# Block-sparse attention and a gated FFN: only batch 0 dense, three tokens to a partition, keys and queries turned by TensorE

## The chip, the cores and the metric

The kernel runs on one core of a Trainium2 chip. The metric is the device time of one execution in microseconds. A core has TensorE (PE: matmuls, with a separate weight load, PEld), VectorE (DVE), ScalarE (ACT), GpSimd (POOL) and the DMA issuing queue of SyncE (SP); ScalarE and GpSimd can issue DMAs too. Each engine works through its own instructions in the order in which they stand in the program, and waits on semaphores for the others. A DMA issue also waits for an older DMA that used the same semaphore, whichever engine issued that one.

## The reference

Attention over 4 batches, 8 heads, 768 tokens and 64 features per head; tokens are grouped in 24 blocks of 32. A query block sees its neighbours (one block to each side), the first and the last block, and three sampled blocks of its own. The first and the last query block see everything. Then an RMS norm and an FFN with a gate over all 3072 tokens:

```
mask = abs(blk_i - blk_j) <= 1  |  blk_i, blk_j in {0, 23}  |  sampled
attn = softmax(where(mask, q @ k.T / 8, -1e9));  o = attn @ v
x  = o as [3072, 512];  xn = x / rms(x) * rms_g
y  = (silu(xn @ w_gate) * (xn @ w_val)) @ w_out      # 512 -> 1536 -> 512
```

Inputs and output are float32; the kernel's matmuls take bfloat16.

## The kernel before

Two ways to do attention stand beside each other. A *dense* batch (`dk`, `dexp`, `dav`, `dxo`; L322, L343, L357, L370) computes all 768 x 768 scores of a head, with the mask added by 24 extra rows of the contraction (88 rows in all). A *sparse* batch computes, for each group of four query blocks (n = 0 to 4; n = 5, `AT`, is the group of the two full rows and two more blocks), the scores against gathered keys only (`qk` L599, `qka` L615, `exp` L605, `expa` L623, `av` L648, `xo` L659). `NDB = 2` batches are dense, two are sparse.

Keys and queries must have features on partitions. Batch 0's are turned by TensorE (`tpx`, L301) and evicted by `evx`. Batch 1's are cast into AUG and turned by a DMA transpose that SP issues (`turn`, L288). The sparse batches are loaded with a key or value layout of two tokens to a partition (`load_kv`, L452, 512-byte runs) and a query layout of one (`load_q`, L459, 256-byte runs), cast (`fill_k`, `fill_v`, `fill_q`) and turned by DMA transposes (`turn_k` L478, `turn_q` L504).

For each group of query blocks the keys are collected in a tile `kg`: neighbours and ends by `kg_fixed` (VectorE or ScalarE), sampled blocks by `kg_sampled` (POOL, L146), at places held in registers (`table`, `table_regs`, `k_at`). Values go to DRAM once in bfloat16 rows (`store_v`, L508) and come back by `pair_v` (L570 to L578, SP) and, for each sampled block, `block_v` (L555: two of three on SP, one on ScalarE).

The FFN takes units of 128 or 384 tokens (`UNITS`): `sq`, `rsq` (POOL, L686), `xq` (L693), then a turn of xn by TensorE for the first `NPET = 6` units (`tr` L704, `cp`) or by a DMA transpose (`xt`, L715), then gate and value projections (`proj`, L728), `th` (tanh on ScalarE, L737), `uu` and `hp` (VectorE, L743, L754) and the output projection `yy` (L767), `yo`, `so`.

The order is not written by hand: all steps are listed by `op(...)` with the engines that may do them, a cost for each, what they depend on, a priority and the buffers and PSUM banks that they take and give back. A greedy planner at the end of the function takes the step that can start first by those costs and issues its instructions. So the planner decides each engine's program order, and for some steps the engine. PSUM banks 0 to 3 in pairs serve scores, 4 and 5 gate and value projections, 6 the output projection, 7 attention output.

Of the kernel before, what the change touches and what calls it, by code (L numbers as in the profile page):

```python
# [10 lines left out]
I32 = mybir.dt.int32  # L11
# [5 lines left out]
def kernel(  # L17
# [33 lines left out]
    NSLOT, NAUG, NOPEN, NDB = 5, 2, 2, 2  # L51
    IXAT, RGAT = 36.0, 48.0
    NPT, NPA, NKG, NVG, NRAW = 4, 2, 2, 3, 3
    AHEAD, HURRY, HURU = 0.8, ("av", "xo", "sq", "rsq", "xq", "tr", "cp"), 0
    NSTARV, ZPAT, NG2 = 3, 32.0, 4
    AH = {"uu": 0.3, "hp": 0.3}
    WARM = (11, 10, 2)
    HD = NC * D // 2
    UNITS = [(0, 0, 1), (0, 1, 1), (0, 2, 1), (0, 3, 3)]
    UNITS += [(b, c, 3) for b in range(1, NDB) for c in (0, 3)]  # L60
    ND = len(UNITS)
    for b in range(NDB, B):
        UNITS += [(b, (5, 0, 1), 3), (b, (2, 3, 4), 3)]
    NU = len(UNITS)
    HG = [("h", 0 if u < 3 else u) for u in range(NU)]
    HO = [u if u < 3 else 0 for u in range(NU)]
# [9 lines left out]
    def bank16(n):  # L76
# [12 lines left out]
    VAC = const.tile([P, 2, H * NC, D + 2], BF16, name="VAC")  # L89
    VGC = const.tile([P, 6, VW], BF16, name="VGC")  # L90
# [6 lines left out]
    RAWD = list(A)  # L97
    RAWS = [RAWC[:, i * RB:(i + 1) * RB] for i in range(NRAW)]
    aug = [AUG[:, i] for i in range(NAUG)]
    va_ = [VAC[:, i] for i in range(2)]  # L100
    vfl = [t.rearrange("p m d -> p (m d)")[:, 0:6 * VW] for t in va_]
    VAUG = [t.rearrange("p (t c h d) -> p t c h d", t=NC // 2, c=2, h=H) for t in (vfl[0], PTC[:, 10240:10240 + 6 * VW])]
    rt_ = RAWC[:, NRAW * RB:].bitcast(BF16)
    VGB = [VGC, rt_[:, 0:6 * VW].rearrange("p (x w) -> p x w", w=VW),
           vfl[1].rearrange("p (x w) -> p x w", w=VW)]
    PD = [PTC[:, i * PDW:(i + 1) * PDW] for i in range(3)]
    PTB = [t.rearrange("p (h l x) -> p h l x", h=2, l=2) for t in [rt_[:, 6 * VW:6 * VW + 1024]] + [
        PTC[:, i * 1024:(i + 1) * 1024] for i in range(NPT - 1)]]
    PAB = [PTC[:, 3072 + i * 2048:3072 + (i + 1) * 2048].rearrange("p (l h x) -> p l h x", l=2, h=2) for i in range(NPA)]
    KTB = [t.rearrange("p (a s) -> p a s", a=NP) for t in (xs_[3], xs_[1])]  # L110
    QTB = [t.rearrange("p (a s) -> p a s", a=NP) for t in (xs_[4], PTC[:, 7168:7168 + NP * S])]
    KGB = [xs_[i].rearrange("p (x a s j c) -> p x a s j c", x=6, a=NP, s=4, j=16) for i in (0, 2)]
    KROW = AUG[:, 0].rearrange("p i e c x -> p (i e c x)").rearrange(
        "p (a c t x) -> p a c t x", a=NP, c=2, t=NC // 2)
    QROW = AUG[:, 1].rearrange("p i e c x -> p (i e c x)").rearrange("p (a n x) -> p a n x", a=NP, n=NC)
    kvv = [t.rearrange("b h (t p c) d -> b p (h t) (c d)", p=P, c=2) for t in (k, v)]
    qvv = q.rearrange("b h (n p) d -> b n p h d", p=P)
# [32 lines left out]
    zt = const.tile([P, VW], BF16, name="zt")  # L150
# [36 lines left out]
    nc.gpsimd.memset(zt[0:32, P:VW], 0.0)  # L187
# [9 lines left out]
    for t in va_:  # L197
        nc.vector.memset(t[:, :, D:D + 1], 1.0)
# [72 lines left out]
    def load(g, i):  # L271
        b, pr = divmod(g, NP)
        if i == 0:
            rawd[g] = RAWD[held["rawd", g][1]]
        nc.sync.dma_start(out=rawd[g][:, i], in_=(kv, qv, vv)[i][b, :, 2 * pr:2 * pr + 2, :])

    def fill(g, i, eng):
        copy(eng, aug[g % NAUG][:, i, :, :, 0:D],
             rawd[g][:, i].rearrange("p h (c d) -> p h c d", d=D))

    def pad_v(g, eng):
        b, pr = divmod(g, NP)
        src = rawd.pop(g) if b else A[g]
        copy(eng, va_[b][:, 2 * pr * NC:2 * (pr + 1) * NC, 0:D],
             src[:, 2].rearrange("p h (c d) -> p (h c) d", d=D))

    def turn(g):
        nc.sync.dma_start_transpose(  # L288
            out=X[g % NSLOT].rearrange("p i e (c t) -> p (i e c) t", t=P),
            in_=aug[g % NAUG].rearrange("p i e c r -> p (i e c r)"))  # L290

    def zero_pad(i):
        nc.vector.memset(aug[i][:, :, :, :, KQ:P], 0.0)
# [15 lines left out]
    held, rawd = {}, {}  # L309
# [38 lines left out]
    def dav(u, pr, bk):  # L348
        b, c0, nt = UNITS[u]
        pt, va = pts.pop((u, pr)), va_[b]  # L350
# [23 lines left out]

    tab_, at_ = VGB[0].rearrange("p x w -> p (x w)"), [0]

    def small(n, dt, p=P):
# [7 lines left out]
    kti, vti = small(NS * 2, I32, 1), small(NS * NR, I32, 1)  # L385
    koff, voff = {}, {}

    REGS = {"POOL": [("k", 0, 16), ("k", 16, 32), ("k", 32, 2 * NS)], "SP": [("v", 0, 16), ("v", 16, 32), ("v", 32, 2 * NS)],
            "ACT": [("v", 2 * NS, 2 * NS + 11), ("v", 2 * NS + 11, 3 * NS)]}
    HALF = 1024  # L390

    def load_table():
        nc.sync.dma_start(
            out=stab.rearrange("p n r i -> p (n r i)"), in_=s64.rearrange("n x -> (n x)").unsqueeze(0))
        for b in range(NDB, B):
            for lo in (0, S + 32):
                nc.sync.dma_start(out=vrows[b][lo:lo + 32, :], in_=zt[0:32, :])

    def table(i, eng):
# [3 lines left out]
        elif i == 1:  # L403
            TC(out=sf, in_=stab[:, 1:NB - 1, :, 0])
            TS(out=d2, in0=sf, scalar1=16.0, scalar2=None, op0=ALU.mult)
            TC(out=kti[:, 0:NS], in_=d2[:, :, 0])
            TS(out=d1[:, :, 0], in0=d2[:, :, 2], scalar1=float(HALF), scalar2=None, op0=ALU.mult)
            TT(out=kti[:, NS:2 * NS], in0=d1[:, :, 0], in1=d2[:, :, 1], op=ALU.add)
# [14 lines left out]
        else:  # L423

            TS(out=d2, in0=sf, scalar1=-1.0, scalar2=float(NB), op0=ALU.mult, op1=ALU.add)
# [6 lines left out]
    def table_regs(eng, part):  # L432
# [5 lines left out]
        for i_, x in enumerate(got_):  # L438
            r, n = divmod(lo + i_, NS)
            {"k": koff, "v": voff}[w][n * NR + r] = x  # L440
# [882 lines left out]
```

## Time and profile before

| what | value |
|---|---|
| median of 3 runs | 308.0 us (307.23 to 308.08) |
| profiled execution | 307.95 us, span 306.2 us |
| granted TensorE clock, mean | 0.989 |
| busy: PE, PEld, DVE, ACT, POOL | 284.4, 183.4, 195.1, 175.2, 80.3 us |
| HBM read, written | 36.70 MB, 8.02 MB |
| DMA packets on queue 1 | 76946, of them 256 B: 43008 |

How to read it: the span is the time from the first to the last instruction on the core; the profiled execution's own time is a little longer. Busy times of an engine count its instructions; register, branch, semaphore and DMA-issuing instructions are not among them. A line of the groups has the line of the kernel, the engine, the operation, out<-in with shapes, count, busy time and mean time of one. A line of the chain has start, length, engine, tile and line. A line of the waits has the engine and line, what it waited for, the total, the number of waits and the longest. A line of the windows has the stretch, its length, busy time of PE, PEld, DVE, ACT and POOL with counts, the granted clock, the DMA share and GB/s. A line of the timeline has start, length, engine, line, operation, tile and count, and in brackets the idle time before and what ended it.

### The profile page before, as it was taken

What the parts mean: (1) busy time and instruction counts of PE and PEld (TensorE: products, weight loads), DVE (VectorE), ACT (ScalarE), POOL (GpSimd) and SP (SyncE); (2) the same over time, 40 slices, a digit from 0 to 9 for tenths busy, and PEclk for the clock granted to TensorE, in tenths of its full rate; (3) what the DMA queues carried; (4) which work ended last, traced back from release to release, by engine and by line L of the source; (5) the groups of instructions that cost most, each with busy time, mean ns of one, the idle gap of its engine ahead of it and who ended that gap; (6) DMA issues with size and microseconds to landing.
All of it is one profiled execution on the core that took longest, in us unless ns stands there. A gap on an engine that the chain in (4) does not pass through costs nothing.

```text
span 306.2 us, 9818 instructions
## 1 busy us (share of the span) xinstructions
PE 284.4 (93%) x3838; PEld 183.4 (60%) x3838; DVE 195.1 (64%) x462; ACT 175.2 (57%) x290; POOL 80.3 (26%) x196
## 2 busy tenths in 40 slices
PE   8999989889999998999779699998699999999995
PEld 7899877666666664665445345564255655546543
DVE  6688896576756755877568435767177958807700
ACT  4899874468888785368554226877065424413322
POOL 4648100010024615119754200755041000100000
PEclk9999999999999999999999979999989999999999
DMA  7999999864799996783987973333754400060032
GB/s 218 364 242 157 203 268 323 182 229 80 119 267 266 182 308 161 159 239 87 263 196 187 195 157 97 90 84 89 166 127 135 92 36 2 0 156 0 1 98 109
DMA packets 85204, 48.50 MB, mean 158 GB/s; under 512 B 48037, under 2 KB 81318, under 8 KB 85158
## 3 DMA queue, kind: packets, MB, share of 16 engines
q1 hardware_dynamic: 76946, 41.63, 54.7%
q0 software_dynamic: 5792, 4.72, 10.1%
q10 hardware_dynamic: 2420, 1.53, 2.0%
q8 instruction: 30, 0.49, 0.6%
q14 instruction: 16, 0.13, 0.1%
HBM read 36.70 MB, written 8.02 MB: 146 GB/s over the span
## 4 chain that ended last, share of the span: by engine, by line
PE 67%; DMA 14%; DVE 8%; issue 5%; SPq 2%; ACT 2%; ACTq 1%; DVEq 0%
PE PS L728 33%; PE PS L767 15%; PE PS L322 7%; PE PS L357 4%; DMA RAWC<-in_v_dram 4%; PE PS L648 3%; DMA XC<-AUG 2%; DMA RAWC<-in_k_dram 2%; PE PS L301 2%; DMA VGC<-vrows 2%; DVE uu L743 2%; PE PS L599 2%; DMA xn<-xq 1%; DVE hp L754 1%; ACT th L737 1%
## 5 line engine op out<-in xcount | busy, mean ns | idle before, releaser
L737 ACT ACTIVATE th<-PS 128x384 bf16<-128x384 f32 x96 | 46.5, 492 | 81.9 <-PE PS L728 37.5
L743 DVE SCALAR_TENSOR_TENSOR uu<-th,PS 128x384 bf16<-128x384 bf16 x96 | 52.4, 551 | 49.4 <-ACT th L737 47.1
L728 PE MATMUL PS<-xn,wg 128*128 128x384 bf16 (+1 forms) x480 | 74.3, 294 | 7.3 <-DVE uu L743 4.2
L343 ACT ACTIVATE PTC<-PS 128x768 bf16<-128x768 f32 x92 | 70.4, 815 | 14.0 <-PE PS L322 13.8
L728 PE MATMUL PS<-xn,wv 128*128 128x384 bf16 (+1 forms) x480 | 77.9, 297 | 0.1
L767 PE MATMUL PS<-wo,hp 128*128 128x512 bf16 (+1 forms) x300 | 71.4, 376 | 4.1 <-DVE uu L743 4.1
L754 DVE TENSOR_TENSOR hp<-uu,PS 128x384 bf16<-128x384 bf16 x96 | 52.0, 551 | 16.8 <-PE PS L728 14.7
L728 PEld LDWEIGHTS <-wg 128*128 128x128 bf16 x480 | 40.7, 98 | 31.4 <-issue 9.0
L146 POOL COPY XC<-XC 128x128 bf16 x132 | 39.3, 371 | 62.6 <-PE PS L599 35.7
L728 PEld LDWEIGHTS <-wv 128*128 128x128 bf16 x480 | 40.5, 98 | 23.9 <-issue 1.9
L767 PEld LDWEIGHTS <-hp 128*128 128x128 bf16 x300 | 29.0, 99 | 32.4 <-issue 6.2
L322 PE MATMUL PS<-XC 88*128 88x128 bf16 (+1 forms) x288 | 42.6, 276 | 0.6 <-ACT PTC L343 0.6
L322 PEld LDWEIGHTS <-XC 88*128 88x128 bf16 x288 | 22.2, 100 | 7.8 <-issue 0.9
L357 PE MATMUL PS<-VAC,PTC 128*128 128x65 bf16 x552 | 21.1, 193 | 0.2 <-DVE XO L370 0.2
L357 PEld LDWEIGHTS <-PTC 128*128 128x128 bf16 x552 | 20.0, 97 | 2.0 <-issue 0.3
L777 ACT ACTIVATE yo<-PS 128x512 f32<-128x512 f32 (+1 forms) x16 | 9.1, 571 | 20.2 <-PE PS L767 20.1
L146 POOL CAST AUG<-RAWC 128x768 bf16<-128x768 f32 (+3 forms) x12 | 11.6, 973 | 30.1 <-DMA RAWC<-in_k_dram 25.7
L693 DVE SCALAR_TENSOR_TENSOR xq<-XO,rs,gB 128x512 bf16<-128x512 f32 x24 | 18.5, 792 | 0.2 <-POOL rs L686 0.2
L686 POOL TENSOR_TENSOR rs<-ms,nhalf 128x1 f32<-128x1 f32 (+1 forms) x6 | 4.3, 714 | 47.8 <-DVE ms L675 47.8
L605 ACT ACTIVATE PTC<-PS 128x1024 bf16<-128x1024 f32 x15 | 15.2, 1022 | 1.6 <-PE PS L599 1.1
L648 PEld LDWEIGHTS <-PTC 128*32 128x32 bf16 x736 | 8.1, 97 | 8.7 <-issue 7.4
L599 PEld LDWEIGHTS <-XC 64*128 64x128 bf16 x480 | 7.5, 93 | 6.9 <-issue 5.8
(112 smaller groups left out, 225.1 us busy)
## 6 DMA issues: line engine op xcount, KB each, us to landing
out_dram<-yo SPq DMA_DIRECT2D x21, 256.0 KB, 2.0
RAWC<-in_k_dram SPq DMA_DIRECT2D x4, 768.0 KB, 5.7
RAWC<-in_v_dram SPq DMA_DIRECT2D x4, 768.0 KB, 10.6
RAWC<-in_q_dram SPq DMA_DIRECT2D x12, 256.0 KB, 5.3
RAWC<-in_v_dram SPq DMA_DIRECT2D x7, 384.0 KB, 6.5
RAWC<-in_k_dram SPq DMA_DIRECT2D x6, 384.0 KB, 6.6
wg<-in_moe_w_gate_dram POOLq DMA_DIRECT2D x4, 384.0 KB, 6.9
wv<-in_moe_w_val_dram POOLq DMA_DIRECT2D x4, 384.0 KB, 7.9
```

The costliest lines, as they stand in the source:

```text
L146: nc.gpsimd.tensor_copy(out=out, in_=in_)
L322: nc.tensor.matmul(out=s_[:, e, j * w:(j + 1) * w], lhsT=x[0:KQ, 0, e, jt * P:(jt + 1) * P], rhs=x[0:KQ, 1, e, c0 * P:c0 * P + w], start=T ...
L343: nc.scalar.activation(out=pts[u, pr][:, g * kt:(g + 1) * kt].rearrange("p j e w -> p e j w"), in_=s_[:, :, 0:kt * w].rearrange("p e (j w) ...
L357: nc.tensor.matmul(out=o_[:, t, e, :], lhsT=pt[:, jt, e, t * P:(t + 1) * P], rhs=va[:, (2 * pr + e) * NC + jt, 0:D + 1], start=(jt == 0), ...
L605: nc.scalar.activation(out=t_.rearrange("p h l x -> p (h l x)"), in_=tiles.pop(("s", b, n, pp)).rearrange("p h l x -> p (h l x)"), func=AF ...
L648: nc.tensor.matmul(out=o_[32 * i:32 * i + 32, a, :], lhsT=l_, rhs=r_, start=i not in begun, stop=k_ == last[i], tile_position=(0, 32 * i), ...
L693: nc.vector.scalar_tensor_tensor(out=xqs[u][:, t, :], in0=xos[u, t].rearrange("p h d -> p (h d)"), scalar=mss[u][:, t:t + 1], in1=gB, op0= ...
L728: nc.tensor.matmul(out=p_[:, j, :].rearrange("p (t w) -> p t w", w=P), lhsT=w_[:, c, f_ * P:(f_ + 1) * P], rhs=xns[u][:, :, c, :], start=( ...
L737: nc.scalar.activation(out=t_, in_=tiles["gp", u, f], func=AF.Tanh, scale=0.5)
L743: nc.vector.scalar_tensor_tensor(out=t_, in0=tiles.pop(("th", u, f)), scalar=1.0, in1=tiles.pop(("gp", u, f)), op0=ALU.add, op1=ALU.mult)
L754: nc.vector.tensor_tensor(out=hps[u][:, f * fg:(f + 1) * fg, :], in0=tiles.pop(("uu", u, f)), in1=tiles.pop(("vp", u, f)), op=ALU.mult)
L767: nc.tensor.matmul(out=tiles["yp", u, t, h], lhsT=hps[u][:, f, t * P:(t + 1) * P], rhs=wo[:, f, x], start=(f == 0), stop=(f == NF - 1))
```

## The change

Batch 1 becomes a sparse batch (`NDB = 1`); batch 0 stays dense. Its dense code path, with its loads, casts, DMA transposes and zero padding, is taken out.

Keys, queries and values of the three sparse batches are all loaded three tokens to a partition, so that a run is 3 x 64 x 4 = 768 bytes, and each of the three tensors comes in two loads of half the heads. After the cast, TensorE turns them, 12 turns of 128x128 into two PSUM banks, and ScalarE evicts them so that tokens stand in natural order again: three neighbouring tokens lay in three different turns, so each eviction writes with a step of three bfloat16 elements, 6 bytes. The key copies that follow then read and write runs of 32 elements instead of two interleaved runs of 16.

The gathers of sampled value blocks are spread over three queues: first on SP, second on ScalarE, third on GpSimd (software DMAs). The registers that hold their places pack several 5-bit block numbers, taken out with a shift and a mask. The sampled-key copies stay on GpSimd; the fixed ones go to VectorE alone. Evictions of turned xn go to ScalarE alone.

FFN units are cut differently: 1, 2, 1, 2 groups in batch 1, then 1, 2, 3, then 3, 3; so gate and value projections also run over 128 and 256 tokens, and small units share one `hp` tile. `NPET = 6` stays, so units from the seventh on have xn turned by DMA. There are four value tiles instead of three and five tiles for exponentials. Buffers share memory differently, and some planner costs and priorities change. The core of the diff:

```diff
-    NSLOT, NAUG, NOPEN, NDB = 5, 2, 2, 2
+    NSLOT, NAUG, NOPEN, NDB = 5, 2, 2, 1
-    NPT, NPA, NKG, NVG, NRAW = 4, 2, 2, 3, 3
+    NPT, NKG, NVG, NRAW = 5, 2, 4, 3
+    SPLIT = (((5,), (0,1), (2,),( 3, 4)), ((5,), (0, 1), (2, 3, 4)), ((5, 0, 1), (2, 3, 4)))
-    UNITS += [(b, c, 3) for b in range(1, NDB) for c in (0, 3)]
-        UNITS += [(b, (5, 0, 1), 3), (b, (2, 3, 4), 3)]
+        UNITS += [(b, ns, len(ns)) for ns in SPLIT[b - NDB]]
...
-    kvv = [t.rearrange("b h (t p c) d -> b p (h t) (c d)", p=P, c=2) for t in (k, v)]
-    qvv = q.rearrange("b h (n p) d -> b n p h d", p=P)
+    kvv = [x.rearrange("b h (t p c) d -> b p (h t) (c d)", p=P, c=NT3) for x in (k, v, q)]
...
-    def turn(g):
-        nc.sync.dma_start_transpose(
-            out=X[g % NSLOT].rearrange("p i e (c t) -> p (i e c) t", t=P),
-            in_=aug[g % NAUG].rearrange("p i e c r -> p (i e c r)"))
...
-    def turn_k(b):
-        KTs[b] = KTB[held["KT", b][1]]
-        nc.sync.dma_start_transpose(
-            out=KTs[b].rearrange("p a (n x) -> p (a n) x", x=P), in_=KROW.rearrange("p a c t x -> p (a c t x)"))
...
+    def turn(b, x, j, bk):
+        t_ = PS[:, bk[0]:bk[0] + 2].rearrange("p b x -> p b x").bitcast(BF16)[:, :, 0:S].rearrange(
+            "p a (c w) -> p a c w", w=P)
+        tiles["turn", b, x, j] = t_
+        for a in range(2):
+            for c in range(NC):
+                nc.tensor.transpose(out=t_[:, a, c, :], in_=(KROW if x == "k" else QROW)[:, 2 * j + a, c, :], identity=ident)
+
+    def turned(b, x, j, eng):
+        ts, tb, n_ = (KTs, KTB, "KT") if x == "k" else (QTs, QTB, "QT")
+        ts[b] = tb[held[n_, b][1]]
+        copy(eng, ts[b][:, 2 * j:2 * j + 2, :].rearrange("p a (t w c) -> p a t c w", w=P, c=NT3),
+             tiles.pop(("turn", b, x, j)).rearrange("p a (t c) w -> p a t c w", c=NT3))
...
-            copy(eng, kg[:, x, :, :, r, :], kt[:, :, :, bass.ds(kb, 16)])
+            copy(eng, kg[:, x, :, r, :], KTs[b][:, :, bass.ds(k_at(blocks(n)[x] - 1, r, eng), 32)])
...
-    def block_v(b, n, x, r):
-        (nc.scalar if r == 2 else nc.sync).dma_start(
-            out=new_vg(b, n)[32 * r:32 * r + 32, x, :],
-            in_=vrows[b][bass.ds(voff[(blocks(n)[x] - 1) * NR + r], 32), :])
+    def block_v(g, n, x, r):
+        (nc.sync, nc.scalar, nc.gpsimd)[r].dma_start(
+            out=new_vg(g, n)[32 * r:32 * r + 32, x, :],
+            in_=vrows[g][32:S + 64, :][bass.ds(v_at(blocks(n)[x] - 1, r), 32), :])
...
+    KFE, SQE, YOE = ("DVE",), ("DVE", "ACT"), ("DVE", "ACT")
+    TTE, TTP = ("ACT",), 0.5
+    KDE, CPE = ("POOL",), ("ACT",)
...
+        for x in "kq":
+            for j in range(2):
+                op(("tt" + x, b, j), {"PE": 12 * 0.056}, [("sf" + x, b, j, c) for c in range(2)], (TTP, b, j),
+                   lambda e, p, a=(b, x, j): turn(*a, p), [(S_, ("tt" + x, b, j))], [(x + "row", b)])
+                op(("turn" + x, b, j), pick_({"ACT": 1.45, "DVE": 1.75}, TTE), [("tt" + x, b, j)], (-0.5, b, j),
+                   lambda e, p, a=(b, x, j): turned(*a, e), [(x.upper() + "T", b)], [(None, ("tt" + x, b, j))])
```

## The prediction, made before the result was known

> **What bounds the kernel now.** I read the page's totals first, then the chain of waits (for the pace of TensorE), then TensorE's timeline (for the holes between its matmuls), the waits, and the other queues.
>
> ```profile
> span 306.2 us, 9818 instructions
> PE 284.4 (93%) x3838; PEld 183.4 (60%) x3838; DVE 195.1 (64%) x462; ACT 175.2 (57%) x290; POOL 80.3 (26%) x196
> ...
> DMA packets 85204, 48.50 MB, mean 158 GB/s; under 512 B 48037, under 2 KB 81318, under 8 KB 85158
> ```
>
> TensorE is busy for 93% of the span; nothing else passes 64%. So time comes from less work on it or from smaller holes. Its pace, from the chain and two lines of its timeline:
>
> ```profile
> 26.22 0.67 PE PS L728 x12
> 83.17 1.30 PE PS L728 x8
> 99.14 1.14 PE PS L357 x36
> 102.23 0.65 PE PS L322 x4
> 103.53 0.65 PE PS L767 x3
> 195.54 0.61 PE PS L615 x36
> 205.88 0.83 PE PS L648 x64
> ...
> 141.74 0.49 PE L599 MATMUL PS<-XC 64*128 64x32 bf16 x24
> 142.16 2.12 PE L767 MATMUL PS<-wo,hp 128*128 128x512 bf16 x9
> ```
>
> Per matmul: 0.056 us for 128 columns, 0.1625 for 384, 0.2165 for 512, 0.0317 for dense weights times values, 0.017 (L615), 0.013 (L648), 0.0175 (L599: 24 start at 141.74, the next line at 142.16). For 256 columns I take 0.109, between 0.056 and 0.1625. Counts times pace: FFN L728 109.2 + 16.1, L767 62.4; dense scores 23.4 + 8.1, dense values 18.3; turns L301 5.4 and L704 2.7; sparse 11.6 + 8.4 + 2.4; warming 2.6. Sum 270.7 us of work. Start to start in the timeline, each start less that pace, the holes sum to 31.8: 5.4 in the first 10 us, 5.9 from 10 to 120 us, 20.5 from 120 to 240, nothing after. The last matmul ends 3.2 before the end; 0.5 is rounding.
>
> ```profile
> ACT th L737 <- DMA VAC<-vrows: 13.4, 2, 10.6
> POOL XC L146 <- DMA XC<-AUG: 8.3, 1, 8.3
> ACT th L737 <- DMA VGC<-vrows: 6.0, 2, 3.5
> ACT th L737 <- DMA XC<-AUG: 5.8, 1, 5.8
> PE PS L728 <- DMA xn<-xq: 3.1, 1, 3.1
> ...
> 160.00:180.00 20.00, 16.71 (x106) 8.57 (x105) 11.34 (x21) 6.99 (x15) 6.08 (x11) 0.92 0.96 205
> 220.00:240.00 20.00, 19.70 (x410) 10.91 (x410) 14.83 (x35) 10.70 (x18) 4.60 (x14) 0.91 0.47 117
> ```
>
> The waits say what the 20.5 is: ScalarE's tanh stands behind ScalarE's own value-gather issues, and these behind an older transfer. At 121 us it was a value load of 11.4 (hole 1.4), at 173 the DMA transpose of keys (holes 3.6), at 217 a transpose of xn (4.4 with its neighbour). 4.7 lies at 144-155 around late score and value groups, 3.4 is granted clock of 0.92 and 0.91 in two 20-us windows (20 x 0.08 + 20 x 0.09), 3.0 is small.
>
> **The change, part by part.**
>
> *TensorE.* Batch 1 becomes sparse: 96 scores of 384 columns go (-15.6), 288 value matmuls go (-9.2). It brings 448 L648 (+5.8), 240 L599 (+4.2), 72 L615 (+1.2). Keys and queries of three batches are turned by 144 matmuls of 128 columns (+8.1); 12 turns of xn move to DMA (-0.7). Cut units make the FFN narrower: 384 x 0.1625 + 288 x 0.109 + 576 x 0.056 = 126.1 against 125.3 (+0.8). Net -5.2, all on the path: 265.5.
>
> *DMA and SP.* Eight DMA transposes of keys and queries go. They held SP's queue for 3.6 to 6.4 us each (34 in all) with loads and gathers behind them, and landed after 6.4. Loads in 768-B runs replace 512- and 256-B ones: 256-B packets fall from 43,008 to 7,680 (the transposes wrote 30,720). SP issues 224 DMAs instead of 233, with 66 gathers for three batches instead of 88 for two. xn transposes rise from 4 to 7, each with the landing that left 3.1 in TensorE's wait.
>
> *ScalarE.* Off: 48 dense exps at 0.81 (-39) and its key copies (16 x 0.48 + 6 x 0.76, -12). On: 14 sparse exps at 1.03 (+14), 12 turning evictions, 22 more gather issues at 0.5 (+11). An eviction of 128x1536 into adjacent addresses took 1.44; writing 6 B apart has no row. Below: 1.35, that copy's pitch; above: 1.9, by the interleaved 512-element copy (0.76) against the plain one (0.58). I take 1.44, the same size and source, +17 in all; the upper end adds 5.5. By program order, from 51 to 184 us of TensorE work ScalarE has 44 tanh (19.6), 36 exps (33.5), 11 evictions (14.9), 62 gathers (31) and 9.8 of the rest: 109 in 133, or 82%. The same count before is 89 in 111, or 80%. A late eviction holds tanh behind it, hence the gate's PSUM bank and the next gate group; it also holds two of the four score banks.
>
> *POOL.* It gets the third gather of each block (66 software DMAs) and a third more key copies. Between the first and last key copy TensorE has 139 us of work, 153 with holes. POOL has 198 copies at 0.257 (51), 22 casts at 0.86 (19), nine rsqrt pairs at 1.1 (10) and 62 DMAs. Such a small software gather has no row: below, 0.5 by SP's gather pitch; above, 1.15, the slowest weight issue on POOL. I take 0.85, the mean there, the same queue: 53. Sum 133 of 153. A gather that waits for its stored rows or a free buffer holds the key copies and rsqrt behind it, and the scores wait for those.
>
> ```profile
> 205.15 1.54 POOL L146 COPY XC<-XC 128x128 bf16 x6
> 208.47 4.35 POOL L146 COPY XC<-XC 128x128 bf16 x12 [1.79 <-PE PS L599]
> ...
> 208.54 2.16 DVE L693 SCALAR_TENSOR_TENSOR xq<-XO,rs,gB 128x512 bf16<-128x512 f32 x3
> ```
>
> The row that speaks against the change: beside VectorE's xq, 12 copies took 0.36 each instead of 0.257. At 0.36 and 1.15 POOL needs 172. The Trainium skill, page "SBUF — State Buffer", section "Who interferes with whom", explains this as one port pair held by whichever engine starts first, and its section on the bandwidth-pool intuition has a software DMA go from about 620 to 3100 ns under a VectorE copy. At 3.1 us for each of the 62, an estimate from that page, POOL would need 272 and the kernel would end near 415; by the rows it is 296. The weight issues of 0.74 to 1.15 here ran beside VectorE casts, so I stay with the rows.
>
> *VectorE.* 63 key copies instead of 20 and more casts. By order it has 41 in 42 us of TensorE work up to the first scores. It hid so far at 34 in 45; if the cover is gone the early holes grow by 1 to 4. I add nothing: before, the same table work ran there with holes of 1.2.
>
> *Cover of batch 1.* Its key turn stands after 48.6 us of TensorE work, some 59 us in. The weight gates that its key loads wait for passed at 32.3 and 36.3; with the slowest landing (10.6) and casts the keys are there at 50. Hidden; without those 9 us TensorE would wait one for one.
>
> *The middle holes.* Of 20.5, the keys' transpose and half of the slow clock go (3.6 + 1.7). The other 15.2 grows with the longer stretch (133/111) to 18.2. With fewer small packets I take a third off, 12.2, and add 2 for POOL's queue: 14. Ends: 6 (only xn landings and small ones) and 24.6 (20.5 x 133/111).
>
> Sum: 265.5 + 11.3 early + 14 + 3.2 + 0.5 = 294.5. The profiled execution took 307.95 for a span of 306.2, 1.75 more; the median of the runs, 308.0, is the same. Prediction 296.3.
>
> **Rivals.** (A) *POOL becomes the bound*, slower: at 172 in 153 it adds 19, some 316. It decides once a gather costs over (153 - 80) / 62 = 1.18 at the fast copy pace, or 0.83 at the slow one. For: nothing else grows so; against: 87% by the middle rows.
> (B) *ScalarE's gather waits stay*, slower: 20.5 of holes for 44 gathers is 0.47 each; 62 make 29, 15 more than I take: 311. It passes the time before at middle holes of 26. For: the 13.4 and 6.0 rows; against: fewer and lighter transfers to stand behind.
> (C) *Nothing relieved*: holes in proportion, 24.6: 307, no change.
> (D) *Planned well*: holes of 6: 288.
> (E) *The evictions don't do what they should* at 1.9: ScalarE 115 of 133; inside B.
>
> **How the numbers follow.** Mine (291 to 302) 0.44, D 0.14, C (303 to 309) 0.16, B with E 0.16, A 0.10. The range must leave out no more than 0.2: below 288 lies 0.05, above 313 some 0.13, so 288 to 313. Given both signs, mine alone is 291 to 302. The measurement tells 0.3% from no change, 307.1 to 308.9: faster is mine, D and half of C, 0.67; same 0.05; slower 0.28.
>
> **What would show it.** TensorE's busy time down by some 5 to 15, no DMA transpose into key or query tiles, evictions near 1.4, POOL gathers near 0.85, POOL between 50 and 65% busy, middle holes near 14 with releasers among gathers and xn. Wrong if the waits name POOL's copies or gathers ahead of scores (A), tanh behind gathers for over 25 us (B), or the first FFN groups stand behind VectorE.

## The result, and the profile after

The changed kernel takes 313.0 us (median; 312.39 to 313.12) against 308.0 us for the kernel before: a ratio of 1.0157, 95% interval 1.0126 to 1.0188. It is 1.6% slower where 3.8% faster was forecast. The ratios here and below leave out slow executions, those over 1.5% longer than the fastest of the same kernel. The profiled execution took 312.39 us, its span is 310.5 us, the mean granted clock 0.978 (before 0.989).

The page's totals, TensorE's busy share and granted clock by fortieths of the span, and the DMA packets:

```profile
span 310.5 us, 12436 instructions
PE 281.0 (90%) x4609; PEld 199.9 (64%) x4634; DVE 205.6 (66%) x506; ACT 168.6 (54%) x230; POOL 135.0 (43%) x348
...
PE   7999789996899397989799999898999999999995
...
PEclk9999959999999897999999999999999999999999
...
DMA packets 58041, 48.09 MB, mean 155 GB/s; under 512 B 14685, under 2 KB 53086, under 8 KB 57982
```

The reader is to see that TensorE has less work and is still the busiest engine by far, that its deepest gaps are the 6 and the 3 of its row (70 to 78 and 101 to 109 us), that the clock fell to half in a slice near 40 us, and that the packets under 512 B went from 48037 to 14685 (those of 256 B on queue 1 from 43008 to 7680, as forecast). So the change did what it says.

I split the span as in the prediction: matmuls times their pace, and the holes between their starts. (25 output projections of the profile after have no record; each is put in at 0.2165 us.)

| us | work | holes 0-10 | 10-60 | 60-120 | 120 on | all holes | rest of span |
|---|---|---|---|---|---|---|---|
| before | 271.0 | 5.4 | 4.5 | 1.1 | 20.8 | 31.8 | 3.4 |
| forecast | 265.5 | 11.3 for both | | 14.0 for both | | 25.3 | 3.7 |
| after | 265.7 | 4.5 | 8.1 | 15.3 | 13.3 | 41.2 | 3.6 |

The forecast's 14 us of "middle holes" belong to the sparse batches. That stretch began near 120 us before; in the forecast it begins after 51 us of TensorE's work, which the changed kernel reaches at 64 us. So 14 stands against 15.3 + 13.3 = 28.6, and the 11.3 of early holes against 12.6.

Against the kernel before, work came down by 5.3 us and the holes from 120 us on by 7.5. That is outweighed by 14.2 us more of holes from 60 to 120 us, where batch 1's dense attention used to stand, and by 3.6 from 10 to 60.

The waits of the page after, as in the prediction's fence: engine, line, what it waited for, total, number, longest.

```profile
POOL RAWC L150 <- DVE RAWC L152: 24.7, 1, 24.7
...
ACT th L706 <- DMA VXC<-vrows: 9.2, 2, 6.8
...
ACT XC L148 <- DMA vrows<-RAWC: 6.7, 1, 6.7
ACT PTC L574 <- DMA VXC<-vrows: 6.7, 1, 6.7
PE PS L697 <- DVE uu L712: 6.2, 5, 4.8
...
ACT XC L148 <- DMA VXC<-vrows: 5.4, 1, 5.4
```

GpSimd stands idle for 24.7 us before batch 1's value casts, ScalarE's tanh (L706) and its turning evictions (L148) stand behind its own value gathers, and TensorE waits for the products after tanh. Pieces of the chain of waits between 58 and 118 us (start, length, what):

```profile
58.61 6.33 DMA vrows<-RAWC
...
65.77 5.12 DMA VXC<-vrows
70.89 2.71 ACT XC L148
...
93.13 10.92 DMA RAWC<-in_k_dram
104.07 0.32 ACTq L524
...
114.59 1.21 POOL AUG L150
115.85 0.84 PE PS L471 x12
```

Batch 1's stored rows land at 64.9; ScalarE's gathers follow, the eviction of keys stands behind them until one of 5.1 us has landed, at 70.89, and TensorE has a hole of 2.2 us there. Batch 2's key load, issued at 93.1, takes 10.9 us to land; ScalarE's next gather, which uses the same semaphore, waits for it until 104.07; tanh stands behind, and TensorE has a hole of 5.0 us at 101. Batch 2's keys are cast only at 114.6 and turned at 115.9, with another hole of 2.4 us behind. This chain first suggested ScalarE; the runs say otherwise.

Groups whose price the prediction had to bound, of ScalarE and GpSimd (line, engine, form, count, busy time, mean ns of one):

```profile
L148 ACT COPY XC<-PS 128x1536 bf16<-128x1536 bf16 x8 | 21.8, 2751 | 15.6 <-DMA vrows<-RAWC 6.7 <-DMA VXC<-vrows 5.4 <-PE PS L471 3.4
...
L150 POOL COPY XC<-XC 128x128 bf16 x198 | 51.8, 308 | 17.5 <-PE PS L568 11.9 <-PE PS L584 3.0 <-ACT XC L148 1.9
L524 POOL DMA_DIRECT2D VXC<-vrows x36 | 18.2, 506 | 6.4 <-issue 3.9 <-DMA vrows<-RAWC 1.2 <-PE PS L568 0.5
```

An eviction that writes 6 bytes apart takes 2.75 us, nearly twice the 1.44 taken and above the upper bound of 1.9. A small software gather takes 0.505, the lower bound. A key copy of GpSimd takes 0.308 on average, between its two rows of before (0.257 and 0.36).

### The profile page after: what moved, and what is told of

The parts are those of the page before. It is cut to its first block, busy times and chain, and to the rows that moved or that the text cites. A ratio compares the mean times of both kernels' runs of the same rounds, so it can differ in the third digit from the quotient of the medians.

```text
span 310.5 us, 12436 instructions
## 1 busy us (share of the span) xinstructions
PE 281.0 (90%) x4609; PEld 199.9 (64%) x4634; DVE 205.6 (66%) x506; ACT 168.6 (54%) x230; POOL 135.0 (43%) x348
## 2 busy tenths in 40 slices
DMA packets 58041, 48.09 MB, mean 155 GB/s; under 512 B 14685, under 2 KB 53086, under 8 KB 57982
## 3 DMA queue, kind: packets, MB, share of 16 engines
q0 software_dynamic: 7904, 6.92, 13.3%
## 4 chain that ended last, share of the span: by engine, by line
PE 54%; DMA 17%; issue 8%; ACT 7%; DVE 7%; SPq 2%; POOL 2%; ACTq 2%; POOLq 1%
PE PS L697 27%; PE PS L736 14%; DMA RAWC<-in_k_dram 5%; DMA wg<-in_moe_w_gate_dram 5%; PE PS L617 4%; ACT XC L148 3%; DMA VXC<-vrows 3%; PE PS L568 3%; PE PS L305 2%; DMA vrows<-RAWC 2%; DVE XC L152 2%; ACTq L524 2%; PE PS L340 2%; ACT VXC L148 1%; DVE uu L712 1%
## 5 line engine op out<-in xcount | busy, mean ns | idle before, releaser
L697 PE MATMUL PS<-xn,wg 128*128 128x128 bf16 (+2 forms) x624 | 76.2, 270 | 11.4 <-DVE uu L712 6.2
L712 DVE SCALAR_TENSOR_TENSOR uu<-th,PS 128x384 bf16<-128x384 bf16 (+1 forms) x90 | 51.8, 579 | 43.5 <-ACT th L706 41.5
L697 PE MATMUL PS<-xn,wv 128*128 128x128 bf16 (+2 forms) x624 | 78.1, 271 | 2.3 <-DMA wv<-in_moe_w_val_dram 1.8
L706 ACT ACTIVATE th<-PS 128x384 bf16<-128x384 f32 (+1 forms) x90 | 45.6, 514 | 58.6 <-PE PS L697 44.8
L697 PEld LDWEIGHTS <-wg 128*128 128x128 bf16 x624 | 50.2, 100 | 28.6 <-issue 11.7
L723 DVE TENSOR_TENSOR hp<-uu,PS 128x384 bf16<-128x384 bf16 (+1 forms) x90 | 50.7, 577 | 20.5 <-PE PS L697 19.4
L150 POOL COPY XC<-XC 128x128 bf16 x198 | 51.8, 308 | 17.5 <-PE PS L568 11.9
L326 ACT ACTIVATE PTC<-PS 128x768 bf16<-128x768 f32 x44 | 33.4, 818 | 4.8 <-PE PS L305 4.6
L148 ACT COPY XC<-PS 128x1536 bf16<-128x1536 bf16 (+1 forms) x9 | 22.2, 2486 | 15.8 <-DMA vrows<-RAWC 6.7
L152 DVE COPY XC<-XC 128x256 bf16<-128x256 bf16 (+1 forms) x63 | 19.9, 362 | 4.0 <-PE PS L568 2.1
L748 DVE TENSOR_SCALAR yo<-PS 128x512 f32<-128x512 f32 (+1 forms) x17 | 11.0, 657 | 17.1 <-PE PS L736 14.7
L305 PE MATMUL PS<-XC 88*128 88x128 bf16 (+1 forms) x192 | 21.7, 249 | 0.6 <-ACT PTC L326 0.6
L524 POOL DMA_DIRECT2D VXC<-vrows x36 | 18.2, 506 | 6.4 <-issue 3.9
L524 POOL DMA_DIRECT2D PTC<-vrows x30 | 15.1, 503 | 7.8 <-issue 5.0
## 6 DMA issues: line engine op xcount, KB each, us to landing
RAWC<-in_k_dram SPq DMA_DIRECT2D x6, 768.0 KB, 10.3
wg<-in_moe_w_gate_dram POOLq DMA_DIRECT2D x4, 384.0 KB, 12.7
```

The costliest lines, as they stand in the source:

```text
L148: nc.scalar.copy(out=out, in_=in_)
L150: nc.gpsimd.tensor_copy(out=out, in_=in_)
L152: nc.vector.tensor_copy(out=out, in_=in_)
L305: nc.tensor.matmul(out=s_[:, e, j * w:(j + 1) * w], lhsT=x[0:KQ, 0, e, jt * P:(jt + 1) * P], rhs=x[0:KQ, 1, e, c0 * P:c0 * P + w], start=T ...
L326: nc.scalar.activation(out=pts[u, pr][:, g * kt:(g + 1) * kt].rearrange("p j e w -> p e j w"), in_=s_[:, :, 0:kt * w].rearrange("p e (j w) ...
L524: (nc.sync, nc.scalar, nc.gpsimd)[r].dma_start(out=new_vg(g, n)[32 * r:32 * r + 32, x, :], in_=vrows[g][32:S + 64, :][bass.ds(v_at(blocks( ...
```

## The experiments

The runs compare by their ratios to the kernel before on the same chip, since its median differed between chips (305.3 to 308.0 us). The number to hold against is 1.0157. "Holes" are counted as in the table above, from each run's own profile.

### Are the evictions at 2.75 us the cause?

```diff
# adjacent writing
-        copy(eng, ts[b][:, 2 * j:2 * j + 2, :].rearrange("p a (t w c) -> p a t c w", w=P, c=NT3),
-             tiles.pop(("turn", b, x, j)).rearrange("p a (t c) w -> p a t c w", c=NT3))
+        copy(eng, ts[b][:, 2 * j:2 * j + 2, :],
+             tiles.pop(("turn", b, x, j)).rearrange("p a c w -> p a (c w)"))
# step on the PSUM side
-... "p a (t w c) -> p a t c w" ... "p a (t c) w -> p a t c w" ...
+... "p a (t w c) -> p a t w c" ... "p a (t c) w -> p a t w c" ...
# on VectorE
-    TTE, TTP = ("ACT",), 0.5
+    TTE, TTP = ("DVE",), 0.5
```

> The changed kernel with one edit: the twelve turning evictions write adjacent addresses, in the order in which the turns left the tokens. Keys and queries so stay permuted and the output is not the reference's; every instruction, its place and its size stay. Theory E (the mis-sized eviction: 2.75 us each instead of 1.44, ScalarE 15.7 us fuller, tanh and score banks held): evictions drop to 1.4 to 1.5, holes between 60 and 240 us fall from 32 by 6 to 13, the time to 300 to 307 us. Rival L (loads, stored rows and gathers land late, and the evictions only fill time that ScalarE would wait anyway): evictions drop as well, but the time stays within 2 us of 313. If the evictions stay at 2.75, the step of 6 bytes is not what costs.

> The changed kernel with the step moved to the other side: an eviction reads the three turns from PSUM in token order and writes adjacent addresses; the same result in the same place. If only scattered writes into SBUF cost, evictions take 1.4 to 1.5 us and the time follows that of adjacent writing (Theory E 300 to 307, Rival L 311 to 315). If any step costs the same, evictions stay at 2.7 to 2.8 and the time at 312 to 314.

> The changed kernel with the twelve turning evictions on VectorE instead of ScalarE, still writing 6 bytes apart; the planner sets the order anew at its 1.75 us for one. VectorE rises from 205.6 by 21 to 33 us busy, ScalarE falls by 33. Theory E: ScalarE was what was too full, VectorE has 60 us free in the middle, so 303 to 309 us. Rival L: 311 to 315. A third way: VectorE's casts and products stand behind the evictions, and it is slower, 316 or more.

Measured: adjacent 1.0127 (1.0070 to 1.0183), read with a step 1.024 (1.0129 to 1.0352), on VectorE 1.062 (1.0528 to 1.0713). The evictions of the first two, and those of VectorE:

```profile
L148 ACT COPY XC<-PS 128x1536 bf16<-128x1536 bf16 x8 | 11.5, 1438 | 18.4 <-DMA PTC<-vrows 8.2 <-DMA VXC<-vrows 7.9 <-PE PS L471 2.2
```

```profile
L148 ACT COPY XC<-PS 128x1536 bf16<-128x1536 bf16 x8 | 11.5, 1439 | 17.9 <-DMA PTC<-vrows 7.1 <-DMA VXC<-vrows 5.9 <-PE PS L471 4.9
```

```profile
L152 DVE COPY XC<-PS 128x1536 bf16<-128x1536 bf16 x8 | 21.9, 2741 | 2.1 <-PE PS L471 2.1
```

So on ScalarE the price is that of writing 6 bytes apart into SBUF; reading PSUM in token order costs nothing. VectorE takes the same 2.74 us for it, but its adjacent write was not run. Taking 15.7 us off ScalarE moved nothing clear of noise: the holes are 41.0 and 40.6 us instead of 41.2. My first theory, the mis-sized eviction, falls; ScalarE only waits longer elsewhere. On VectorE the order is written anew, and the holes are 49.8. One of them, 4.95 us at 70, stands behind a single xq of VectorE that took 5.93 us (its median elsewhere is 0.74) while GpSimd cast and copied without a pause.

### Are the late weights the cause?

```diff
-                gate = 2 + hf if b == NDB and i == 0 else None
+                gate = 2 + hf if b == NDB and i == 1 else None
```

> The changed kernel with the wait for weight parts 2 and 3 put ahead of batch 1's two value loads instead of its two key loads; key and query loads follow them in the queue as before. Theory W (value loads of 1.5 MB beside the weights made these land in 12.7 and 14.8 us instead of 6.9 and 7.9): weights land in 7 to 9 us, holes from 10 to 60 us fall from 8.5 to 4 to 5, and the time by 2 to 4 us to 309 to 311. Rival: values, keys and the first sparse group come as much later, holes move past 60 us, and the time stays at 312 to 315.

Measured: 1.0126 (1.0035 to 1.0216). The landing of the gate weights in the profile after, and here (line, queue, count, KB each, median us):

```profile
wg<-in_moe_w_gate_dram POOLq DMA_DIRECT2D x4, 384.0 KB, 12.7
```

```profile
wg<-in_moe_w_gate_dram POOLq DMA_DIRECT2D x4, 384.0 KB, 8.1
```

The mechanism is as said: the holes from 10 to 60 us fall from 8.1 to 1.4. In the profiled execution (the longest of its four) they come back later (16.9 from 60 to 120, 18.3 after); the time can't be told from that of the changed kernel. Late weights are real and worth at most a few us.

### Are ScalarE's gathers the cause?

```diff
# to GpSimd (to SyncE: nc.sync in both places)
-        (nc.sync, nc.scalar, nc.gpsimd)[r].dma_start(
+        (nc.sync, nc.gpsimd, nc.gpsimd)[r].dma_start(
-        e = {"POOL": nc.gpsimd, "DVE": nc.vector, "ACT": nc.scalar, "SP": nc.sync}[eng]
+        e = {"POOL": nc.gpsimd, "DVE": nc.vector, "ACT": nc.gpsimd, "SP": nc.sync}[eng]
# loads of batches 2 and 3 on GpSimd
-        nc.sync.dma_start(
+        (nc.gpsimd if b > NDB else nc.sync).dma_start(
# none on ScalarE: SyncE's takes 64 rows
-        (nc.sync, nc.scalar, nc.gpsimd)[r].dma_start(
-            out=new_vg(g, n)[32 * r:32 * r + 32, x, :], ...
+        if r != 1:
+            (nc.sync, None, nc.gpsimd)[r].dma_start(
+                out=new_vg(g, n)[32 * r:32 * r + (32 if r else 64), x, :], ...
```

> The changed kernel with one edit: ScalarE's 66 value gathers (and the registers for them) go to GpSimd, in the same places of the order. Evictions stay at 2.75 us. Theory G (ScalarE's gather issues wait for older 768 KB loads, and hold the turning evictions and tanh behind them: 5.4 us at 65 to 71, 6.75 at 98 to 105): ScalarE no longer waits for gathers, the holes at 71 (2.2) and 101 us (5.0) go and some of the later ones, together 8 to 12 us, and the time is 301 to 306 us. Rival P: GpSimd, 135 us busy, takes 33 us more, its gathers wait in turn and hold key copies and rsqrt; holes move to these and the time stays at 310 to 318.

> The changed kernel with ScalarE's 66 value gathers (and their registers) on SyncE's queue instead, in the same places of the order. Theory G: ScalarE's waits for gathers go as well; SyncE takes 33 us more of issues that wait for the same loads, so values come later and part of the gain is lost: 304 to 311 us. Rival Q: the gathers land so much later that TensorE waits for values, 313 to 325.

> The changed kernel with the twelve loads of batches 2 and 3 issued by GpSimd as software DMAs instead of by SyncE, in the same places of the order; gathers stay where they are. Theory G: the gather of ScalarE that waited 6.75 us at 98 to 105 us stood behind a key load of 10.9 us only because both share a queue's order; it goes, with the hole at 101 us (5.0): 306 to 310 us; the wait at 65 to 71 us stays, since batch 1's loads are untouched. Rival M (memory is simply busy, so that gathers land late beside a load): the gathers still land late and the time stays within 2 us of 313. Rival P: GpSimd waits for a free buffer before each load and holds key copies: over 315.

> Three edits at once: gathers of ScalarE on GpSimd, the evictions' step on the PSUM side (1.44 us each), and the weight wait ahead of batch 1's value loads. If the causes are separate, their gains add: 8 to 12 for the gathers, 2 to 3 for the weights, 0 to 2 for the evictions: 297 to 303 us, below the kernel before. If GpSimd takes the place of ScalarE as the engine that holds others: 308 to 315.

> The changed kernel without ScalarE's 66 value gathers: SyncE's gather takes 64 rows instead of 32 in their place (a block wrong and its neighbour), so the values gathered are not those of the reference; all else keeps its place. The two runs before moved these gathers to GpSimd and SyncE and were slower (324 to 333), so whichever queue has them pays. Theory G (the issues with their waits cost 33 us of queue and hold evictions and tanh): without them ScalarE waits for no gather, the holes at 71 and 101 us and some later ones go, 8 to 14 us, and the half-clock stretches that follow the long holes go with them: 297 to 305 us. Rival K (the keys and values of each batch are late by themselves: loads of 10 us, casts, stores; gathers only show it): the hole near 71 stays, the time is 308 to 313.

Measured: on GpSimd 1.0647 (1.0559 to 1.0736), on SyncE 1.086 (1.0789 to 1.0932), loads on GpSimd 1.0269 (1.0179 to 1.0359), the three edits at once 1.0452 (1.0353 to 1.0550), none on ScalarE 1.0245 (1.0166 to 1.0324). Every one is slower than the changed kernel or no faster, and the last one settles theory G (ScalarE's gathers hold tanh and the evictions): with no gather on ScalarE nothing is gained. TensorE then waits near the same places for something else, batch 2's keys (waits of that run):

```profile
POOL AUG L150 <- DMA RAWC<-in_k_dram: 9.7, 4, 4.6
...
PE PS L471 <- POOL AUG L150: 7.5, 2, 4.5
```

That is: TensorE's turn (L471) waits for GpSimd's casts, and these for the key loads. Moved to GpSimd they add 33 us to its queue, and rsqrt comes late (VectorE's xq waits 11.9 us for it in the profiled execution, the longest of the four). Moved to SyncE they hold what stands in that queue: TensorE waits 15.4 us for turned xn and 8.7 for key casts.

The run with the loads on GpSimd needs a second look, since batch 2's loads went out earlier there: from 82.7 us on, the second key load at 95.9, against 92.0 and 109.1 in the changed kernel. It gained nothing. But one of its holes, 4.4 us at 111, stands behind an xq of VectorE that took 6.29 us (median of its 24: 0.745), while GpSimd copied and cast without a pause (GpSimd's and VectorE's lines of that run):

```profile
108.45 2.87 POOL L150 COPY XC<-XC 128x128 bf16 x12
109.06 6.29 DVE L662 SCALAR_TENSOR_TENSOR xq<-XO,rs,gB 128x512 bf16<-128x512 f32 x1
...
112.06 3.43 POOL L150 COPY XC<-XC 128x128 bf16 x12
```

So this run says neither that early loads help nor that they don't.

### What is late, then?

```diff
# values of batch 1 cast on GpSimd alone
-    CE = {1: (DP_, DP_, DP_), 2: (P_,DP_,DP_), 3: (P_,P_,P_)}
+    CE = {1: (P_, DP_, DP_), 2: (P_,DP_,DP_), 3: (P_,P_,P_)}
# keys loaded first
-    WOG, ORD = None, "vkq"
+    WOG, ORD = None, "kvq"
# the kernel before, its sparse batches turned by TensorE
-    PEQ, PEK = (), ()
+    PEQ, PEK = (2, 3), (2, 3)
```

> The changed kernel with one edit: batch 1's four value casts on GpSimd alone (GpSimd stood idle for 24.7 us before them, waiting for VectorE's casts into the same tile, and VectorE came to these at 55 us, behind the table of sampled blocks and the FFN's products). Theory V (this makes the stored rows late, 58.6 us, and so the first gathers and what ScalarE has behind them): the rows are stored by 42 to 50 us, the hole near 71 us goes or falls below 1, time 306 to 310. Rival K (batch 1's second key and query loads, 56.8 to 70 us, are what is late): hole stays, time 311 to 315.

> The changed kernel with each batch's keys loaded first, then values, then queries (before: values, keys, queries); batch 1's key loads keep their wait for weight parts 2 and 3 and now nothing of batch 1 is loaded beside these. Theory W: weights land in 7 to 9 us, the half-clock stretch at 39 to 45 us goes (2 to 4 us gained, as with the moved wait, 310). Theory K (keys late): keys come 15 us earlier, the hole near 71 us falls as well, 304 to 308. Rival: values are then late, TensorE waits for them: 311 to 316.

> The kernel before with one part of the change alone: keys and queries of its two sparse batches are turned by TensorE (96 turns of 128 columns, 5.4 us) and evicted, in its own layouts (adjacent writes of 768 or 512 elements), instead of by four DMA transposes of 4 to 6 us. If those transposes were worth what I took for them (3.6 of holes in the middle, more by the gathers that stood behind them), the gain pays for the turns: 303 to 308 us. If they were hidden, the time rises by the turns and the evictions: 310 to 316 us.

Measured: 1.0581 (1.0532 to 1.0631), 1.0601 (1.0529 to 1.0674), and 1.0070 (1.0034 to 1.0106) for the kernel before with turns by TensorE.

The first two don't answer their question. GpSimd's value casts still began only at 51.5 us, and the rows were stored at 56.9 instead of 58.6; keys loaded first let the weights land in 7.5 us, with holes of 3.1 from 10 to 60 us, but 23.7 from 60 to 120. In both the whole order was new, with holes of 53.7 us. The third is clean: 5.4 us more work for TensorE cost 0.7%, 2.1 us. So, by difference, the four DMA transposes were worth some 3 us, and that does not pay for the turns in their place.

### SyncE's queue and the landing of the loads

In the changed kernel, SyncE's queue around batch 2's loads (start, length of the stretch, line, tile, number of issues; L524 sampled gathers, L539 and L541 fixed ones, L449 loads):

```profile
86.33 5.56 SPq L524 DMA_DIRECT2D PTC<-vrows  x8
91.99 1.05 SPq L449 DMA_DIRECT2D RAWC<-in_v_dram  x2
93.13 1.35 SPq L449 DMA_DIRECT2D RAWC<-in_k_dram  x1
94.53 4.31 SPq L539 DMA_DIRECT2D VXC<-vrows  x2
98.93 0.64 SPq L541 DMA_DIRECT2D VXC<-vrows  x1
99.92 4.65 SPq L524 DMA_DIRECT2D VXC<-vrows  x4
...
106.71 2.32 SPq L524 DMA_DIRECT2D VXC<-vrows  x4
109.13 0.41 SPq L449 DMA_DIRECT2D RAWC<-in_k_dram  x1
```

Batch 2's first load stands behind 14 sampled gathers of batch 1 at some 0.65 us each, and its second key load is issued 16 us after the first. Before, a dense batch 1 had no gathers; batch 2's key and value loads went out between 84.7 and 92.0 us, and its first scores stood at 132.9. Now the second turn of batch 2's keys, at 115.9, waits for keys whose load was issued 6.7 us earlier.

```diff
# one gather of 96 rows, on GpSimd
-        (nc.sync, nc.scalar, nc.gpsimd)[r].dma_start(
+        if r == 2:
+            nc.gpsimd.dma_start(out=new_vg(g, n)[0:96, x, :], ...
# loads of batches 2 and 3 at half their bytes
+        nh = HH * NC // NT3 // (2 if b > NDB else 1)
-            out=raws[key].rearrange("p (h y) -> p h y", y=NT3 * D),
+            out=raws[key].rearrange("p (h y) -> p h y", y=NT3 * D)[:, 0:nh],
# none on SyncE: ScalarE's takes 64 rows
+        if r:
+            (None, nc.scalar, nc.gpsimd)[r].dma_start(
+                out=new_vg(g, n)[0 if r == 1 else 64:32 * r + 32, x, :], ...
```

> The changed kernel with one value gather per block instead of three: GpSimd's takes 96 rows, SyncE's and ScalarE's 66 each are not issued, so the values gathered are not those of the reference; the bytes are the same. Theory Q (SyncE's queue is what is late: loads of the next batch stand behind gathers that wait): batch 2's second key load is issued near 95 instead of 109 us, holes from 60 to 240 us fall from 32 to under 20, 295 to 303 us. Rival D (the landing of loads, with casts and turns in a row, sets the pace of each batch): 308 to 314.

> The changed kernel with the twelve loads of batches 2 and 3 at half their bytes (half of the heads; keys, queries and values of these batches are not those of the reference); the instructions stay. Theory D: loads land in 5 instead of 10 us, casts and turns of batches 2 and 3 come 4 to 5 us earlier each, the holes at 101 and 118 us fall by 4 to 8 with the half clock behind them: 302 to 308 us. Theory Q: issue times stay as they are, the time stays within 2 us of 313.

> Both at once: one gather of 96 rows per block, and half the bytes in the loads of batches 2 and 3 (neither is the reference's). If queue and landing are two parts of one chain that sets the pace, both together give more than each: 290 to 300 us, near the 270 us of work and 11 us of early holes. If the order of the program sets it (casts, products and turns behind each other on their engines), 304 us or more even so.

> The changed kernel without SyncE's 66 value gathers: ScalarE's takes 64 rows in their place, so the values gathered are not those of the reference; ScalarE's and GpSimd's stay. Theory Q (SyncE's queue alone): batch 2's first loads are issued near 78 to 82 us instead of 92 to 93, its second key load near 97 instead of 109; 299 to 304 us, as without both. Theory QG (both queues together, each with the same loads to stand behind): 306 to 311 us, since ScalarE's waits stay. If 311 to 314, neither queue alone is the cause.

| run | ratio | 95% interval | holes 60-120 | 120 on | all | batch 2's first load, second key load |
|---|---|---|---|---|---|---|
| changed kernel | 1.0157 | 1.0126 to 1.0188 | 15.3 | 13.3 | 41.2 | 92.0, 109.1 |
| no gather on ScalarE | 1.0245 | 1.0166 to 1.0324 | 14.7 | 14.6 | 39.9 | 89.9, 105.9 |
| ScalarE's on SyncE too | 1.0860 | 1.0789 to 1.0932 | 19.7 | 31.4 | 61.0 | 93.9, 112.7 |
| no gather on SyncE | 0.9914 | 0.9868 to 0.9959 | 12.2 | 8.1 | 30.3 | 80.0, 98.3 |
| neither | 0.9851 | 0.9831 to 0.9872 | 10.1 | 8.0 | 28.3 | 77.8, 96.8 |
| loads halved | 1.0007 | 0.9961 to 1.0052 | 11.7 | 12.5 | 33.9 | 89.7, 102.2 |
| neither, and loads halved | 0.9822 | 0.9792 to 0.9852 | 9.4 | 8.7 | 27.7 | 76.8, 94.5 |

This is the main cause of the loss. With 132, 66 and no sampled gathers in SyncE's queue the ratio is 1.086, 1.016 and 0.991, while those of ScalarE, taken away alone, give nothing; so it is not the number of DMAs. The step from 66 to 132 is another matter than the one from none to 66: it moves batch 2's loads by only 2 to 4 us, and TensorE's long waits there are for turned xn. Without SyncE's gathers, batch 2's loads go out 12 us earlier:

```profile
80.02 1.60 SPq L449 DMA_DIRECT2D RAWC<-in_v_dram  x2
84.78 0.37 SPq L449 DMA_DIRECT2D RAWC<-in_k_dram  x1
...
98.28 0.54 SPq L449 DMA_DIRECT2D RAWC<-in_k_dram  x1
```

ScalarE waits as long for its gathers as before in that run (8.0, 5.8 and 5.6 us are its longest three), and the time falls all the same. Halving the bytes (landing 5.2 instead of 10.3 us for keys) is worth 1.5%. Both together give 0.3% more than taking the gathers away alone, as two links of one chain would.

That the gathers cost their 2.4% through batch 2's loads is likely, not shown. For it speak the run without ScalarE's gathers, where TensorE waits 7.5 us for casts that wait for these loads, and the halved loads, though halving also takes traffic from everything else. The gathers' absence lets values land earlier too, and what part that is was not separated. In the two runs where the loads alone went out early (on GpSimd, and loads first below), other waits came and nothing was gained.

### Versions with the right result

```diff
# measured landings for the planner (with the moved weight wait and the step on the PSUM side)
-    DLAT = {"turnk": 3.0, "turnq": 3.0, "st": 2.5, "l": 4.0, ...
+    DLAT = {"turnk": 3.0, "turnq": 3.0, "st": 4.0, "l": 8.0, ...
# loads of batches 2 and 3 ahead of gathers (with the step on the PSUM side)
-                op(("l",) + key, ..., [("w", gate)] if gate else [], (1,), lkv, ...
+                op(("l",) + key, ..., [("w", gate)] if gate else [], (1,) if b == NDB else (-0.6,), lkv, ...
```

> The changed kernel, result as the reference's, with the planner told what was measured: 8 us instead of 4 from a load's end to its data, 4 instead of 2.5 for the stored rows; evictions with their step on the PSUM side (1.44 us, as the planner has it), and the weight wait ahead of batch 1's values. The order is written anew. Theory O (the order was written for loads of 4 us, so turns and score groups stand ahead of work that was ready): TensorE gets ready FFN work first, holes from 60 to 240 us fall by 8 or more from 32, 300 to 307 us. Rival: the same delays show elsewhere, 309 to 318, as in the other runs that had the order written anew.

> The changed kernel with the same result and two edits: loads of batches 2 and 3 stand ahead of gathers in the planner's priority (batch 2's first loads stand behind 4 pairs and 42 fewer gather rows of the program order), and evictions have their step on the PSUM side (no effect on the time in its own run). Theory Q: loads of batch 2 are issued near 75 to 82 us and TensorE's holes from 60 to 240 us fall from 32 to 20 to 26: 302 to 309 us. Rival: the values that the first groups wait for come later by as much, or the new order brings other waits, as in five runs before: 311 to 325.

Measured: 1.0468 (1.0431 to 1.0505) and 1.0571 (1.0471 to 1.0671). In the second, loads went out as early as hoped (69.1 to 78.2 us, the second key load at 90.6), and the holes grew to 51.7 us, 25 of them after 120: TensorE waited 4.4 us at 85 for gathered values, which now stood behind the loads; ScalarE's evictions stood 12.7 us behind an output store by way of a gather, its output copies 10.2 us. Five kernels had most of their order written anew (this one, VectorE's evictions, the two of batch 1, the planner's landings), and all lost 3 to 5% against the changed kernel; why was not followed in each (VectorE's xq of 5.93 us, above, is one reason in one of them). No version with the right result beat the kernel before. Whether one exists is open; the runs without SyncE's gathers show the room, 2 to 3% of the changed kernel.

## Why the prediction was wrong

**The step that failed** is *The middle holes*: of the 20.5 us of before, the transpose and half the slow clock were taken off, the rest was stretched to 133 us of TensorE's work, a third was taken off for fewer small packets, 2 was added for GpSimd's queue, and 14 was left. It was 28.6, and these 14.6 us are nearly all of the 16 by which the span missed (310.5 against 294.5). The packets did fall to a third; the holes did not follow them.

What the step left out is what stands ahead of batch 2's loads. *DMA and SP* counted SyncE's issues over the whole kernel (224 instead of 233, as it came) and called it relief. A dense batch 1 issued no gathers, so none stood ahead of batch 2's loads; now 14 sampled gathers stand ahead of the first and 22 ahead of the second key load. Without SyncE's 66 gathers the holes from 60 us on are 20.3 instead of 28.6, so some 8 of the 14.6 go with them; with ScalarE's away as well they are 18.1, and halving the loads too leaves them there. What the rest is stays open.

*Cover of batch 1* was off in its times, but that cost little. It took the weight gates at the times of before (32.3 and 36.3). The value loads of batch 1 now run ahead of the gates, beside the weights, which land in 12.7 us instead of 6.9. So the gates passed at 38.5 and 54.9, and the second half of the keys was loaded at 56.8, not there at 50. Yet the two turns began at 61.1 and 68.2, where some 59 was forecast, with holes of only 0.2 us from 60 to 70; 3.2 us of holes follow at 71 and 75. The late weights gave 3.6 us more of holes from 10 to 60, and moving the wait repaired these without a clear gain in time.

**Right.** TensorE's net of -5.2 (its terms as listed add up to -5.4): by counts and paces it came to -5.3, and 256 columns, taken at 0.109 us, went at 0.109. The early holes of 11.3: 12.6. No DMA transposes of keys and queries, small packets down to a third. Rival A fell: GpSimd is busy for 43%, gathers at 0.505 (its threshold at the slow copy pace comes to 0.85, not 0.83, and neither was reached).

**Right by luck.** Rival B came nearest, in time (311) and in middle holes (29 against 28.6), but by the wrong cause: it priced ScalarE's waits for its gathers. These stayed (up to 6.8 us), and taking all its gathers away gained nothing.

**Mis-sized, without effect here.** The eviction, 1.44 taken and 2.75 measured: the bounds came from copies with other patterns, and its upper end of 1.9 was still too low. ScalarE's 15.7 us more lay beside other work. The small gather was taken at 0.85 and GpSimd at 50 to 65% busy; both were less.

**Right in size.** DMA transposes: priced at 3.6 us of holes and 1.7 of clock; in the kernel before, taking away four was worth some 3 us, by difference.

**Not priced as an effect of holes.** The prediction carried the granted clock as a loose 3.4 us, inside the middle holes, and took half of it off. In the profile after it is 6.8 us (0.022 of 310.5), again counted in the holes. The half-clock stretches follow holes, as the last section shows.

## What to carry to other kernels

Before work that hides something is taken out, list what it hid on every queue, not only on the engine it ran on: here a dense batch issued no gathers, so none stood ahead of the next batch's loads. Count issues by what stands behind them, not in total, and follow each load from its place in the queue to the first matmul that needs it. A wait at the end of a chain (ScalarE behind its gathers) is not the cause until taking it away moves the time.

## What the runs showed of the hardware

A write of bfloat16 from PSUM into SBUF 6 bytes apart takes 2.75 us for 128x1536 on ScalarE and 2.74 on VectorE; adjacent it takes 1.44 on ScalarE, and reading PSUM with the step instead also 1.44.

A run of GpSimd instructions can, it seems, hold one of VectorE's. Two xq of 128x512 took 6.29 us (loads on GpSimd) and 5.93 us (evictions on VectorE) instead of some 0.75, each while GpSimd copied and cast one instruction after another, and each ended within 0.6 us of the last of these copies. Each time TensorE had a hole behind it, of 4.4 and 4.95 us. At 208.5 us of the kernel before, three xq and 12 copies overlapped as well, and there it was the copies that took longer (0.36 instead of 0.257); no run isolates what decides.

A hole of TensorE can cost more than its length. The windows of 1 us around the hole at 118 us of the changed kernel (stretch, length, busy time of PE, PEld, DVE, ACT and POOL with counts, granted clock, DMA share, GB/s):

```profile
118.00:119.00 1.00, 0.14 (x11) 0.02 (x2) 0.73 (x3) 1.00 (x1) 0.69 (x3) 1.00 1.04 333
119.00:120.00 1.00, 0.00 (x0) 0.00 (x0) 0.00 (x0) 0.47 (x1) 0.00 (x0) 1.00 1.09 341
120.00:121.00 1.00, 0.58 (x6) 0.58 (x7) 0.00 (x0) 0.00 (x0) 0.51 (x1) 0.70 1.08 298
121.00:122.00 1.00, 1.00 (x13) 1.00 (x11) 0.00 (x0) 0.08 (x1) 1.00 (x2) 0.50 0.87 200
122.00:123.00 1.00, 1.00 (x11) 0.89 (x9) 0.56 (x1) 1.00 (x2) 0.09 (x1) 0.50 0.39 89
123.00:124.00 1.00, 1.00 (x58) 0.82 (x56) 0.73 (x2) 0.32 (x1) 0.42 (x1) 0.60 0.29 49
```

TensorE was idle for 2.28 us; then the clock was halved from 120.4 to 123.8 (0.70 and 0.60 are windows partly slow), so another 1.7 us were lost. The same followed the hole at 101 us (106.7 to 110.2), and for twice as long the holes from 36 us (38.5 to 45.3). Not every hole is followed so: 1.99 us of idle at 71.7 was not, nor 2.40 us at 69.0 in the run without SyncE's gathers. The kernel with 61.0 us of holes (SyncE's queue with 132 gathers) has a clock of 0.953, the one with 30.3 (none) 0.994. The Trainium skill, page "TensorE: Matmul & The Clock Gate", Part 1, describes a gate that halves the clock after an idle window of about 3.4 us and opens after a busy one; the lengths of 3.4 and 6.8 us agree with that, the idle time of 2.28 us was shorter than the page says is needed.
